# Where q and k of one chunk are turned: by the DMA crossbar behind their load, or on TensorE

## The chip, the cores and the metric

The kernel runs on one core of a Trainium2 chip. The metric is the time of one execution on the device, in microseconds (us). The kernel before was run 11 times: the median is 215.7 us, the lowest 214.82 and the highest 217.98. A difference is given against that median.

The core has five engines, each with its own queue of instructions, which it runs in order: PE (TensorE: matmuls, and transposes as matmuls against an identity matrix), DVE (VectorE), ACT (ScalarE), POOL (GpSimd) and SP (SyncE, which here only issues DMAs). All DMAs share 16 DMA engines. A DMA transpose is a DMA that writes its source turned (rows to columns)[...].

## The reference

A decayed linear attention feeds a feed-forward layer. B=4 batches, H=8 heads, S=768 positions, D=64; the layer has 512 inputs and 2048 hidden units.

```
gamma = 1 - 2 ** (-5 - arange(H))
for t in range(S):
    state = gamma * state + einsum('bhd,bhe->bhde', k[:, :, t], v[:, :, t])
    y[:, :, t] = einsum('bhd,bhde->bhe', q[:, :, t], state) / sqrt(D)
x = y with the heads side by side, 3072 tokens x 512
h = x @ w_in                      # 512 -> 2048
g = h + sin(alpha * h) ** 2 / (alpha + 1e-9)
out = g @ w_out                   # 2048 -> 512, f32
```

## The kernel before, in words

**Chunks.** Positions are cut in chunks of 128; each batch has 6, so there are 24. The list `P` gives the order of work: first the first chunk of each batch (`e0` to `e3`, which are P[0] to P[3]), then the others, batch by batch. P[4] to P[8] are the rest of batch 0, P[9] begins the rest of batch 1. The change is about P[7], the eighth in this order.

**What a chunk goes through.** Its q, k and v are loaded by POOL, three DMAs that cast f32 to bf16 on the way (`load_chunk`, line 83); v is multiplied by decay factors (`scale_v`, line 137). For the scores, q and k have to lie with the head dimension on partitions, so both are transposed: 128 rows of 2 x 512 values become the tile `qkT`. There are two ways for this in the kernel:

- `stage_T` (lines 246 to 251): eight TensorE transposes of 128x128 into one PSUM bank with the tag "ty", and one copy from PSUM to `qkT` on DVE or ACT.
- `turn` (line 256): one DMA transpose, issued by SP, from the loaded tile `qkr` to `qkT`. SP waits for both loads (q and k) before it issues it.

`qkT` has 6 buffers, taken in turn by either way. Then `stage_A` (line 265) computes the scores in small matmuls and DVE masks them (line 269, tile `aT`); `stage_M` (lines 299 and 303) computes the outputs from the state and the scores, adds the chunk to the state (line 279, kept by ACT at line 286), and DVE writes the result to `xT` (line 310). Chunks of the later batches use another layout ("wide") with functions of their own; all of them are turned by DMA.

**Groups and phases.** The feed-forward layer takes the chunks in groups of 4, 2, 4, 4, 4, 4 and 2. A hidden slot (class `Slot`) is matmuls with `w_in` (line 425, tile `ph`), a sine and a square on ACT (lines 428 and 433), and an addition on DVE (line 440, tile `gT`). Matmuls with `w_out` (line 450, tile `po`) of the group before are laid between. A finished tile of 128 tokens is copied by ACT (line 462) and stored by an SP DMA (line 463, `out_dram`). A group's first `ph` matmul needs `xT` of all its chunks.

**Around the change.** The order on each engine is the order in which the code is written (a manual schedule). While the feed-forward of group 1 runs (`phase(1, ...)`, eight steps n = 0 to 7 of two slots each), the attention of P[6] to P[9], which make group 2, is spread over its steps:

```
    phase(1, outs,
          {0: [X(P[8])], 1: [A(P[6])], 2: [T(P[7]), X(P[9])], 3: [A(P[7]), M(P[6])], 4: [X(P[10])],
           5: [A(P[8]), M(P[7])], 6: [X(P[11]), A(P[9]), M(P[8]), SK(e1)], 7: [M(P[9])]}, 2)
```

X is `turn`, T is `stage_T`, A is `stage_A`, M is `stage_M`. So of these four chunks P[6], P[8] and P[9] are turned by DMA and P[7] on TensorE. P[6]'s `turn` is written before the last `w_out` matmuls of the tiles 0 and 1. SP's queue before is: the turn of P[6], the stores of output tiles 0, 1 and 2, then the turns of P[8], P[9], P[10] and P[11], the store of tile 3, and so on. POOL's queue has the loads of P[7], P[8], P[9] and so on, with scalings of v between them, each of which waits for its v.

Of the kernel before, what the change touches and what calls it, by code (L numbers as in the profile page):

```python
# [15 lines left out]
def kernel(  # L16
# [52 lines left out]
    def chunk_of(t, j):  # L69
        b, c = divmod(j, NCH)  # L70
        return t[b, :, c * C:(c + 1) * C, :].rearrange("h s d -> s h d")

    def load_chunk(j, names="qkv"):
        for name, src in (("q", q), ("k", k), ("v", v)):
            if name not in names:
                continue
            if name == "v":
                t = big.tile([128, H, D], BF16, name="vr", tag="vr", bufs=NJ - 9)
            else:
                if ("qk", j) not in raw:  # L80
                    raw["qk", j] = big.tile([128, 2, H, D], BF16, name="qkr", tag="qkr", bufs=NJ - 10)
                t = raw["qk", j][:, "qk".index(name)]
            nc.gpsimd.dma_start(out=t, in_=chunk_of(src, j))  # L83
            raw[name, j] = t

    def wide(j):
        return j >= 2 * NCH + 2 and j != 3 * NCH
# [45 lines left out]
    def scale_v(j, eng):  # L133
        t, by = raw["v", j], kg
        if wide(j):
            t, by = t.rearrange("i f p d -> i (f p) d"), kgq
        eng.tensor_mul(t, t, by[:, j % NCH, :, None].to_broadcast([128, H, D]))  # L137
# [103 lines left out]
    def stage_T(j, eng=None, tag="ty"):  # L241
        pt = psum.tile([128, 2 * NP, 128], BF16, name="pt", tag=tag, bufs=4 if tag == "mm" else 1)
        st["qkT", j] = work.tile([128, 2 * NP, 128], BF16, name="qkT", tag="qkT", bufs=6)
        for i in range(2):
            for p in range(NP):
                nc.tensor.transpose(pt[:, i * NP + p, :],
                                    raw["qk"[i], j][:, 2 * p:2 * p + 2, :].rearrange("p h d -> p (h d)"), ident)
        if eng is nc.scalar:
            nc.scalar.copy(st["qkT", j], pt)
        else:  # L250
            nc.vector.tensor_copy(st["qkT", j], pt)

    def turn(j):

        st["qkT", j] = work.tile([128, 2 * NP, 128], BF16, name="qkT", tag="qkT", bufs=6)
        nc.sync.dma_start_transpose(out=st["qkT", j], in_=raw["qk", j].rearrange(
            "i a f p d -> i (a f p d)" if wide(j) else "i a h d -> i (a h d)"))

    def stage_A(j):
        qkT = st["qkT", j]  # L260
        pa = psum.tile([128, 2, NP, 128], F32, name="pa", tag="pa")
        for p in range(NP):
            for e in range(2):
                r = slice(64 * e, 64 * e + 64)
                nc.tensor.matmul(pa[:, e, p, :], qkT[r, NP + p, :], qkT[r, p, :],  # L265
                                 start=(p == 0), stop=True, skip_group_check=True)
        aT = work.tile([128, 2, NP, 128], BF16, name="aT", tag="aT", bufs=2)
        m = dec.rearrange("p e n t -> p (e n) t") if j % NCH == 0 else mask_bc
        nc.vector.tensor_mul(aT.rearrange("p e n t -> p (e n) t"), pa.rearrange("p e n t -> p (e n) t"), m)  # L269
        st["aT", j] = aT  # L270
# [17 lines left out]
    def stage_M(j):  # L288
        c = j % NCH
        g, i = place[j]  # L290
        if g not in xT:
            xT[g] = work.tile([128, KS, sizes[g] * C], BF16, name="xT", tag="xT", bufs=3)
        qkT, aT, vs = st["qkT", j], st["aT", j], raw["v", j]
        py = psum.tile([128, NP, 128], F32, name="py", tag="ty")
        if c > 0:
            for p in range(NP):
                for e in range(2):
                    r = slice(64 * e, 64 * e + 64)
                    nc.tensor.matmul(py[r, p, :], s_bd[c % 2][:, p, r], qkT[:, p, :],  # L299
                                     start=(p == 0), stop=True, skip_group_check=True)  # L300
        for p in range(NP):
            for e in range(2):
                nc.tensor.matmul(py[64 * e:64 * e + 64, p, :], vs[:, 2 * p + e, :], aT[:, e, p, :],  # L303
                                 start=(c == 0 and p == 0), stop=True, skip_group_check=True)
        x = xT[g][:, :, i * C:(i + 1) * C]
        if c == 0:
            nc.scalar.copy(x, py)
            return
        ps = stage_S(j) if c < NCH - 1 else None
        nc.vector.tensor_mul(x, py, qg[:, c])  # L310
        if ps is not None:
            keep_S(j, ps)
# [229 lines left out]
    def phase(g, outs, att, nf=1):  # L542


        no, done = len(outs), 0
        for n in range(FF // nf):
            more, fresh = rest[0], {}
            now = Slot(g, n * nf, nf=nf).sq("A")
            run(more, "keep", "exit", "hand")
            for fn in att.get(n, ()):  # L550
                fresh.update(fn() or {})
            run(fresh, "mask")
            if fresh:
                rest[0] = fresh
            now.add()
            while done < no * (n + 1) * nf // FF:
                outs[done]()
                done += 1

    def T(j):  # L560
        return lambda: stage_T(j)

    def X(j):
        return lambda: turn(j)

    def A(j):
        return lambda: stage_A(j)

    def M(j):
        return lambda: stage_M(j)  # L570

    def SK(j):
        return lambda: keep_S(j, stage_S(j))
# [3 lines left out]
    P = order  # L577
# [82 lines left out]


    load_chunk(P[7])
    load_chunk(P[8])
    scale_v(P[6], nc.gpsimd)
    load_chunk(P[9])
# [24 lines left out]
    def fill(n):  # L690
        for _ in range(n):
# [9 lines left out]
    stage_M(P[5])  # L701
    fill(4)
    phase(1, outs,
          {0: [X(P[8])], 1: [A(P[6])], 2: [T(P[7]), X(P[9])], 3: [A(P[7]), M(P[6])], 4: [X(P[10])],
           5: [A(P[8]), M(P[7])], 6: [X(P[11]), A(P[9]), M(P[8]), SK(e1)], 7: [M(P[9])]}, 2)

    where = {10: (2, 1)}
# [69 lines left out]
```

## Time and profile before

| | |
|---|---|
| median of 11 runs | 215.7 us |
| the profiled execution | 215.21 us |
| its span, from the first to the last instruction | 213.4 us |
| what lies around the span | 1.8 us |
| TensorE clock granted | 1.00 |
| PE busy | 201.9 us (95%) |
| ACT busy | 159.8 us (75%) |
| DVE busy | 132.1 us (62%) |
| POOL busy | 103.4 us (48%) |
| DMA queue of POOL (loads) | 13.38 MB, 77360 packets |
| DMA queue of SP (transposes, stores) | 11.28 MB, 23808 packets |
| DMA transposes | 17, of which 8 from `qkr` and 9 from the wide tiles |

The page of a profile has a row of busy tenths for each engine over 40 equal slices of the span (here 5.3 us each), a row for the DMA engines, the chain of work that ended last, and the groups of instructions with their durations. Finer views list instructions in order of time, with the idle time before one and what ended it ("0.29 <-DMA qkT" means 0.29 us idle until a DMA into qkT landed). PEld is the weight load that goes ahead of each matmul; SPq marks an instruction of SP's queue. A DMA's duration in such a list is the issuing engine's time alone; the time to landing is given apart.

### The profile page before, as it was taken

The numbers are of one execution on the slowest core, as the hardware profiler recorded it, in microseconds if no ns is written. First come the engines' busy times: TensorE is split into PE (matmuls) and PEld (weight loads), VectorE is DVE, ScalarE is ACT, GpSimd is POOL, SyncE is SP. The second block draws the span as 40 slices with busy tenths as digits, with TensorE's granted clock in tenths as the row PEclk, the third lists the DMA queues.
The fourth block names the chain that finished last, engine by engine and source line by source line (L and its number), as shares of the span: only waits on it lengthen the run. The fifth ranks groups of instructions, "written<-read, shape, count | busy, mean of one in ns | idle before, by whom it ended". The sixth has DMA issues, their size and how long they took to land.

```text
span 213.4 us, 4667 instructions
## 1 busy us (share of the span) xinstructions
PE 201.9 (95%) x1822; PEld 109.1 (51%) x1849; DVE 132.1 (62%) x250; ACT 159.8 (75%) x302; POOL 103.4 (48%) x136
## 2 busy tenths in 40 slices
PE   7898999899989999999999999999999999999994
PEld 2444554457664555554554554554545444665653
DVE  4787859975896777756655756765744644433311
ACT  7688696758889998897697787677678687766630
POOL 8975434899679969999995103303300100000000
PEclk9999999999999999999999999999999999999999
DMA  9999999999999999999999343141011101111112
GB/s 129 146 183 183 206 207 176 154 144 231 169 140 207 127 148 195 93 185 173 173 146 164 92 98 79 22 101 51 0 51 52 48 1 52 49 49 52 49 49 98
DMA packets 101189, 24.95 MB, mean 117 GB/s; under 512 B 93728, under 2 KB 98224, under 8 KB 101168
## 3 DMA queue, kind: packets, MB, share of 16 engines
q0 software_dynamic: 77360, 13.38, 82.4%
q1 hardware_dynamic: 23808, 11.28, 25.0%
q8 instruction: 14, 0.23, 0.4%
q14 instruction: 7, 0.06, 0.1%
HBM read 27.27 MB, written 6.29 MB: 157 GB/s over the span
## 4 chain that ended last, share of the span: by engine, by line
PE 80%; DVE 8%; ACT 7%; issue 3%; DVEq 0%; ACTq 0%
PE po L450 33%; PE ph L425 33%; ACT s L428 4%; DVE aT L269 3%; PE spare L491 3%; DVE gT L440 2%; ACT s L433 2%; PE pa L265 2%; PE poh L473 2%; PE py L299 1%; PE py L303 1%; PE pa L337 1%; PE py L327 1%; DVE xT L310 1%; PE ps L279 1%
## 5 line engine op out<-in xcount | busy, mean ns | idle before, releaser
L440 DVE SCALAR_TENSOR_TENSOR gT<-s,rec_alpha,ph 128x512 bf16<-128x512 f32 (+3 forms) x120 | 74.3, 638 | 64.6 <-ACT s L433 64.3
L425 PE MATMUL ph<-xT,w_in 128*128 128x512 bf16 (+3 forms) x479 | 97.9, 336 | 0.6 <-DVE gT L440 0.2
L428 ACT ACTIVATE s<-ph,alpha_sb 128x512 f32<-128x512 f32 (+3 forms) x120 | 69.5, 601 | 33.8 <-PE ph L425 33.5
L450 PE MATMUL po<-w_out,gT 128*128 128x512 bf16 x343 | 90.6, 379 | 3.3 <-issue 2.5
L425 PEld LDWEIGHTS <-w_in 128*128 128x128 bf16 x480 | 45.6, 98 | 41.9 <-issue 1.1
L433 ACT ACTIVATE s<-s 128x512 f32<-128x512 f32 (+1 forms) x94 | 58.4, 621 | 2.6
L450 PEld LDWEIGHTS <-gT 128*128 128x128 bf16 x368 | 33.9, 98 | 36.4 <-issue 0.6
L391 POOL CAST s_bd<-s_f 64x256 bf16<-64x256 f32 x10 | 3.9, 394 | 40.3 <-DVE s_f L384 30.1
L462 ACT COPY o_sb<-po 128x512 f32<-128x512 f32 x23 | 13.2, 579 | 4.0 <-PE po L450 3.9
L83 POOL DMA_DIRECT2D vr<-in_v_dram x15 | 13.7, 914 | 3.0 <-DMA w_in<-in_moe_w_in_dram 1.7
L83 POOL DMA_DIRECT2D qkr<-in_q_dram x14 | 12.8, 913 | 3.9 <-DMA w_out<-in_moe_w_out_dram 1.7
L137 POOL TENSOR_TENSOR vr<-vr,kg 128x512 bf16<-128x512 bf16 x12 | 12.7, 1072 | 4.0 <-DMA vr<-in_v_dram 3.5
L83 POOL DMA_DIRECT2D qkr<-in_k_dram x14 | 12.5, 892 | 4.0 <-DMA w_out<-in_moe_w_out_dram 3.3
L269 DVE TENSOR_TENSOR aT<-pa,mask 128x1024 bf16<-128x1024 f32 x11 | 13.4, 1219 | 0.5 <-PE pa L265 0.5
L103 POOL DMA_DIRECT2D qk_seq<-in_q_dram x16 | 11.3, 762 | 1.9 <-DMA vr<-in_v_dram 1.2
L103 POOL DMA_DIRECT2D v_seq<-in_v_dram x16 | 11.3, 796 | 0.0
L137 POOL TENSOR_TENSOR v_seq<-v_seq,kgq 128x512 bf16<-128x512 bf16 x9 | 9.6, 1107 | 3.6 <-DMA v_seq<-in_v_dram 3.3
L103 POOL DMA_DIRECT2D qk_seq<-in_k_dram x16 | 11.3, 775 | 0.0
L491 PE MATMUL spare<-warm 128*128 128x512 bf16 x27 | 9.7, 482 | 1.3 <-DVE warm L156 1.2
L286 ACT CAST s_bd<-ps 64x256 bf16<-64x256 f32 x24 | 8.7, 361 | 2.3 <-PE ps L279 2.1
L346 DVE TENSOR_TENSOR aTw<-pa,maskq 128x768 bf16<-128x768 f32 x9 | 8.6, 954 | 0.7
L310 DVE TENSOR_TENSOR xT<-py,qg 128x512 bf16<-128x512 f32 x11 | 7.5, 684 | 1.2 <-PE py L303 1.2
(92 smaller groups left out, 142.8 us busy)
## 6 DMA issues: line engine op xcount, KB each, us to landing
out_dram<-o_sb SPq DMA_DIRECT2D x23, 256.0 KB, 2.3
w_in<-in_moe_w_in_dram POOLq DMA_DIRECT2D x4, 512.0 KB, 11.2
w_out<-in_moe_w_out_dram POOLq DMA_DIRECT2D x4, 512.0 KB, 14.9
vr<-in_v_dram POOLq DMA_DIRECT2D x15, 128.0 KB, 6.9
qkr<-in_q_dram POOLq DMA_DIRECT2D x14, 128.0 KB, 7.0
qkr<-in_k_dram POOLq DMA_DIRECT2D x14, 128.0 KB, 7.0
qk_seq<-in_q_dram POOLq DMA_DIRECT2D x8, 80.0 KB, 6.3
qk_seq<-in_k_dram POOLq DMA_DIRECT2D x8, 80.0 KB, 4.4
```

The source lines that it names most:

```text
L83: nc.gpsimd.dma_start(out=t, in_=chunk_of(src, j))
L103: nc.gpsimd.dma_start(out=o, in_=src[bt, h, cs[0] * C:, :].rearrange("(f i) d -> i f d", i=64))
L137: eng.tensor_mul(t, t, by[:, j % NCH, :, None].to_broadcast([128, H, D]))
L269: nc.vector.tensor_mul(aT.rearrange("p e n t -> p (e n) t"), pa.rearrange("p e n t -> p (e n) t"), m)
L310: nc.vector.tensor_mul(x, py, qg[:, c])
L425: nc.tensor.matmul(self.ph[:, m, :], w_in[:, i, f * 128:(f + 1) * 128], xT[g][:, i, self.lo:self.hi], start=(m == 0 and i == 0), stop=(i = ...
L428: nc.scalar.activation(out=self.s[:, m, :], in_=self.ph[:, m, :], func=ACTF.Sin, scale=alpha_sb[:, f:f + 1])
L433: nc.scalar.activation(out=self.s, in_=self.s, func=ACTF.Square)
L440: nc.vector.scalar_tensor_tensor(gT[self.g][:, f, self.lo:self.hi], self.s[:, m, :], rec_alpha[:, f:f + 1], self.ph[:, m, :], op0=ALU.mult ...
L450: nc.tensor.matmul(po[g, ts], gT[g][:, f, ts * C:(ts + 1) * C], w_out[:, f, :], start=(f == 0), stop=(f == FF - 1))
L462: nc.scalar.copy(o_sb, po[g, ts])
L491: nc.tensor.matmul(spare["ps"], warm[:, :128], warm, start=True, stop=True)
```

## The change

P[7] is turned by a DMA transpose that SP issues, written right behind the chunk's loads. The TensorE transposes and the DVE copy of step n = 2 are left out. The order of the others stays as it was.

```diff
     load_chunk(P[7])
+    turn(P[7])
     load_chunk(P[8])
     scale_v(P[6], nc.gpsimd)
...
     phase(1, outs,
-          {0: [X(P[8])], 1: [A(P[6])], 2: [T(P[7]), X(P[9])], 3: [A(P[7]), M(P[6])], 4: [X(P[10])],
+          {0: [X(P[8])], 1: [A(P[6])], 2: [X(P[9])], 3: [A(P[7]), M(P[6])], 4: [X(P[10])],
            5: [A(P[8]), M(P[7])], 6: [X(P[11]), A(P[9]), M(P[8]), SK(e1)], 7: [M(P[9])]}, 2)
```

On PE this takes out eight transposes with their weight loads, on DVE one copy of 128x1024. On SP one DMA transpose comes in, after the stores of tiles 0 and 1 and before the store of tile 2, which is followed by the turn of P[8]. POOL's and ACT's queues are the same as before. P[7] takes the second buffer of `qkT` and P[8] the third; before, it was the other way round.

## The prediction

> **What bounds the kernel now.** I read the page first, then the chain of work that ended last, then what stands in front of the instructions around the change, last the DMA engines. The page:
>
> ```profile
> PE 201.9 (95%) x1822; PEld 109.1 (51%) x1849; DVE 132.1 (62%) x250; ACT 159.8 (75%) x302; POOL 103.4 (48%) x136
> ...
> DMA  9999999999999999999999343141011101111112
> ```
>
> PE is the bound of the whole, at 95%. The DMA engines are busy in every slice of the first 22, until 117 us. The change sits at 46 to 65 us, in that part: there a transfer takes its time from another.
>
> The chain, in order of time, from P[7]'s present transpose to the start of group 2 (start, duration, what):
>
> ```profile
> 52.55 0.78 DVE gT L440 x2
> 53.33 0.61 DVE qkT L251
> 53.94 0.05 issue
> 53.99 0.40 PE pa L265 x8
> ...
> 63.96 0.65 DVE xT L310
> 64.61 0.04 issue
> 64.65 1.02 PE ph L425 x4
> ```
>
> Phase 1 is a chain through DVE, PE and ACT and not PE work end to end; it ends with P[9]'s `xT`, behind which PE begins group 2 at 64.65. From there PE fills the time (4.00 of 4.00 us in the stretch from 66 to 70), so what phase 1 ends later, the kernel ends later. What PE's queues wait for in it, from the timeline:
>
> ```profile
> 53.99 0.40 PE L265 MATMUL pa<-qkT 64*128 64x128 bf16 x8 [0.22 <-DVE qkT L251]
> 57.80 0.23 PEld L265 LDWEIGHTS <-qkT 64*128 64x128 bf16 x8 [0.29 <-DMA qkT<-qkr]
> 60.61 0.23 PEld L265 LDWEIGHTS <-qkT 64*128 64x128 bf16 x8 [0.59 <-DMA qkT<-qkr]
> ```
>
> These are the scores of P[7], P[8] and P[9]. The last two wait for their DMA transposes: these land at the last moment. SP's own timeline has the issues, to which I add the time to landing that each has when it is asked for alone:
>
> ```profile
> 49.24 1.28 SPq L256 DMA_TRANSPOSE qkT<-qkr  x1
> ...
> 54.01 1.23 SPq L256 DMA_TRANSPOSE qkT<-qkr  x1
> ```
>
> P[8]: 49.24 + 8.5 = 57.75, used at 57.80. P[9]: 54.01 + 6.56 = 60.57, used at 60.61. Slack 0.05 and 0.04 us. P[6] (43.15 + 6.7 = 49.85) is used at 50.20. Later ones have more: P[10] 1.7 us, P[13] 1.6, P[15] 0.9, from P[16] on over 6.
>
> **What goes away.** Eight PE transposes: 0.61 us as modelled, 0.45 from the first to the next matmul (51.85 to 52.30). The DVE copy: 0.69 us, of which 0.61 on the chain. Without both, PE could start P[7]'s scores behind the `ph` matmuls before them, 0.45 earlier than these end now (53.77), at about 53.3 and not 53.99: 0.7 us at most. [...] The row shows them pipelined at 0.45, and the row decides. Whichever it is, this time can't reach the end: the scores of P[8] wait for a DMA at 57.75 that nothing here brings forward. So the saving counts as 0; were P[8] and P[9] not held by DMA, it would be worth up to 0.7.
>
> **What comes in: SP's part.** P[7]'s k is issued at 38.83 and lands 6.9 us later, at 45.8; SP has issued the store of tile 1 by 45.9. The turn starts there and holds SP for 1.24 us, to 47.1. Behind it stands the store of tile 2, which is ready only at 48.74, and then P[8]'s turn. So SP's queue is covered by 1.6 us; a k landing later than that would push the store and P[8]'s turn by the excess. POOL's queue is not changed. The `qkT` buffers that P[7] and P[8] now take belonged to e1 and e2, read long before.
>
> **What comes in: the DMA engines' part.** On SP's DMA queue the new transpose lies behind P[6]'s (landing 49.85) and the stores of tiles 0 and 1 (landing 51.2) and ahead of the store of tile 2 and of P[8]'s transpose. These engines have no room:
>
> ```profile
> 50.00:54.00 4.00, 3.62 (x40) 2.57 (x39) 3.46 (x7) 3.53 (x8) 3.55 (x4) 1.00 2.01 220
> 54.00:58.00 4.00, 3.83 (x59) 2.94 (x60) 3.22 (x6) 3.34 (x9) 2.65 (x3) 1.00 1.97 156
> ```
>
> Behind the stretch stand its length, the busy time of PE, PEld, DVE, ACT and POOL with instructions in brackets, and the granted clock; the last two columns are the busy share of the DMA engines (over 1, since packets overlap on an engine) and GB/s. From 54 to 58 us only loads and a transpose ran, 156 GB/s. A transpose writes 128 x 1024 x 2 bytes = 0.262 MB: 0.262 / 156 GB/s = 1.7 us of all engines. One q load (0.131 MB) is 0.8 us by the same rate.
>
> Ends for its cost. Upper: P[8]'s and P[9]'s transposes, both queued, land 2.8 us apart (57.75, 60.57), which is a transpose and about one load between. [...] even alone, at 131 us, a transpose takes 3.1 us from issue to landing with 1.3 of it on SP. I take 2.1 us: the 1.7 of the transpose and half of a load that gets its turn in between. It is nearer to the 1.7 row, which is the same kind of DMA in the same stage.
>
> **Where the delay goes.** P[7]: its transpose follows the stores at 51.2, so it lands at about 53 to 54.5 (its fellows take 6.4 to 8.5 us from issue, which from 45.9 is 52.3 to 54.4). Its scores start between 53.3 and 54.5: at best 0.7 gained, at worst 0.5 lost, both hidden by the next wait. P[8]: lands at 57.75 + 2.1 = 59.85, the scores start 2.05 later than now. PE stands there, and in its queue behind it stand `M` of P[7], `po` matmuls and the `ph` of step 6; ACT and DVE run dry with it. P[9]: its transpose lies behind P[8]'s, so 60.57 + 2.1 = 62.7. From its scores to the start of group 2, PE's order (scores, `M` of P[8], two `po`, eight `ph`, `M` of P[9], `xT`) takes 64.65 - 60.61 = 4.04 us as now. Group 2 starts at 66.7, 2.0 later. The loads behind are late by about as much as PE is, so P[10] and later keep their slack.
>
> **Sum.** Saving 0, delay +2.0: 215.2 + 2.0 = 217.2 for the profiled execution. This stands 0.5 under the median of the runs, so 215.7 + 2.0 = 217.7 us.
>
> **The rivals.** *Absorbed, no change (the other side).* On the 16 engines the new transpose may take its turn from loads rather than from P[8]'s transpose, for example in the dip at 47.4 to 48 us, where the engines moved half as much. It decides at P[9]'s landing: under 1.1 us later, no difference can be told; unmoved, the 0.7 us saved at P[7] still end at the wait for P[8], and the time is 215.0 to 216.5. For it: P[9]'s loads have slack of their own, and the dip. Against it: one queue in order, P[8] behind P[7], and slack of 0.05.
>
> *Faster.* Only if P[8] and P[9] landed earlier too, with the saving of 0.7 passed on, and a later PE gap closed: 214.5. Nothing in the order of SP or POOL does that.
>
> *More than the transpose.* A load more gets ahead at each turn (the 2.8 us row), POOL, which waits for v before it loads on, falls behind PE, and the chunks with little slack (P[13], P[15] with 0.9) wait a second time: 2.8 + 0.5 to 1, so 219.0 to 219.5.
>
> *Late at P[7] itself.* P[8] needs 3.8 us behind P[7]'s scores (53.99 to 57.80). P[7] would have to land after 56.1 to be what holds P[8] at 59.85. It ends at the same time, 217.7 to 218.5, by another wait.
>
> **How the numbers follow.** P[8] and P[9] pushed by 1.1 to 2.8 us: 0.58. More than that: 0.10. Late at P[7]: 0.07. Absorbed: 0.18. Faster: 0.07. A measurement of this kernel tells 0.5%, 1.1 us, from no change. Slower by over that: 0.58 + 0.10 + 0.07 = 0.75; within it 0.18; faster 0.07. The range goes from 215.5, an absorbed case, to 219.3; the likeliest case's own is 216.8 to 218.6.
>
> **What would show it.** Right: no L246 on PE and no L251 on DVE at 52 to 54; a ninth DMA transpose from `qkr`, issued at about 45.9; P[8]'s scores at about 59.9 and P[9]'s at 62.7, both with an idle wait for the DMA into `qkT`, in sum some 2 us more of it; `ph` of group 2 at 66.7; the same spans behind it. Wrong: P[9]'s scores at 60.6 or earlier, or a start of group 2 at 64.65 or earlier (absorbed), new DMA waits of PE after 70 us (more than the transpose), or P[8]'s scores late without a wait of their own for a DMA (late at P[7]).

## The result and the profile after

The changed kernel takes 218.44 us in the median of 12 runs, against 215.53 us for the kernel before beside it (47 runs). The ratio is 1.0119, with a 95% interval of 1.0096 to 1.0143, and leaves out three of the 12 runs, of 220.6 to 221.1 us, as slow. By this ratio the change costs 2.6 us (2.1 to 3.1). The profiled execution took 218.54 us, its span is 216.8 us (213.4 before).

The page of the changed kernel, first its engines, then the DMA engines over the 40 slices, then the chain that ended last, by engine and by line:

```profile
PE 200.8 (93%) x1814; PEld 107.9 (50%) x1841; DVE 131.2 (61%) x249; ACT 160.1 (74%) x302; POOL 103.4 (48%) x136
...
DMA  9999999999999999999999940331011011111112
...
PE 72%; DMA 14%; POOL 4%; ACT 4%; issue 2%; DVE 2%; POOLq 0%; DVEq 0%; ACTq 0%
PE po L450 32%; PE ph L425 31%; DMA qkT<-qkr 7%; DMA qkr<-in_k_dram 5%; DMA qkT<-qk_seq 2%; POOL qkr L83 2%; ACT s L428 2%; PE poh L473 2%; PE pa L265 2%; PE py L299 1%; POOL vr L83 1%; PE pa L337 1%; PE py L303 1%; PE py L327 1%; ACT s L433 1%
```

PE has eight matmuls fewer and DVE one instruction fewer: the transposes and the copy are gone. The time is longer all the same. The chain now runs through DMAs for 14%, which had no share that the page listed before. Of these, 5% are a load at 10 to 21 us, ahead of anything that differs; the other 9% are transposes into `qkT`. The timeline of PE in the changed kernel has the scores of P[6], P[7], P[8] and P[9], each with its wait:

```profile
52.09 0.40 PE L265 MATMUL pa<-qkT 64*128 64x128 bf16 x8 [0.96 <-DMA qkT<-qkr]
...
56.74 0.40 PE L265 MATMUL pa<-qkT 64*128 64x128 bf16 x8 [1.54 <-DMA qkT<-qkr]
...
60.75 0.40 PE L265 MATMUL pa<-qkT 64*128 64x128 bf16 x8 [0.20 <-DMA qkT<-qkr]
...
63.81 0.40 PE L265 MATMUL pa<-qkT 64*128 64x128 bf16 x8 [0.56 <-DMA qkT<-qkr]
```

All four wait for a DMA transpose. The chain in order of time, from the issue of P[7]'s transpose to the start of group 2:

```profile
47.02 9.68 DMA qkT<-qkr
56.70 0.04 issue
56.74 0.40 PE pa L265 x8
...
58.35 5.42 DMA qkT<-qkr
63.77 0.05 issue
63.81 0.40 PE pa L265 x8
...
66.92 0.70 DVE xT L310
67.62 0.04 issue
67.67 1.02 PE ph L425 x4
```

Two transposes, P[7]'s with 9.68 us and P[9]'s with 5.42, take the place of DVE and ACT work on the chain. P[9]'s is issued at 58.35 and not at 54.01: SP waits for P[9]'s k, which lands 11.5 us behind its own issue (7.8 before). Group 2 starts at 67.67 and not at 64.65. Not all of these 3.0 us belong to the change: this execution was 0.9 us late by the scores of P[4] at 41.16 (40.30 before), ahead of anything that differs. P[6]'s transpose was issued 0.69 us late (43.84, before 43.15). I therefore count from this issue to the start of group 2: 21.50 us before, 23.83 after, 2.3 us more.

The last 0.4 us comes later. Behind 68 us two weight loads of PE wait for a DMA into `qkT`, those of P[13] and P[15]. First the kernel before, then the changed one:

```profile
82.54 0.23 PEld L265 LDWEIGHTS <-qkT 64*128 64x128 bf16 x8 [0.42 <-issue]
94.72 0.11 PEld L337 LDWEIGHTS <-qkT 64*64 64x64 bf16 x4 [0.42 <-issue]
...
85.55 0.23 PEld L265 LDWEIGHTS <-qkT 64*128 64x128 bf16 x8 [0.42 <-DMA qkT<-qkr]
98.15 0.11 PEld L337 LDWEIGHTS <-qkT 64*64 64x64 bf16 x4 [0.84 <-DMA qkT<-qk_seq]
```

PEld stands idle for 0.42 us at both places in the kernel before too, without a DMA. So P[13] loses nothing here (its matmuls have no wait), and P[15] loses 0.4 us. From the start of group 2 to the end of the span it is 149.1 us, before 148.75.

### The profile page after: what moved, and what is told of

It reads as the page before. It is cut to its first block, busy times and chain, and to the rows that moved or that the text cites. A ratio compares the mean times of both kernels' runs of the same rounds, so it can differ in the third digit from the quotient of the medians.

```text
span 216.8 us, 4652 instructions
## 1 busy us (share of the span) xinstructions
PE 200.8 (93%) x1814; PEld 107.9 (50%) x1841; DVE 131.2 (61%) x249; ACT 160.1 (74%) x302; POOL 103.4 (48%) x136
## 4 chain that ended last, share of the span: by engine, by line
PE 72%; DMA 14%; POOL 4%; ACT 4%; issue 2%; DVE 2%; POOLq 0%; DVEq 0%; ACTq 0%
PE po L450 32%; PE ph L425 31%; DMA qkT<-qkr 7%; DMA qkr<-in_k_dram 5%; DMA qkT<-qk_seq 2%; POOL qkr L83 2%; ACT s L428 2%; PE poh L473 2%; PE pa L265 2%; PE py L299 1%; POOL vr L83 1%; PE pa L337 1%; PE py L303 1%; PE py L327 1%; ACT s L433 1%
## 5 line engine op out<-in xcount | busy, mean ns | idle before, releaser
L462 ACT COPY o_sb<-po 128x512 f32<-128x512 f32 x23 | 13.2, 578 | 4.0 <-PE po L450 3.9
L491 PE MATMUL spare<-warm 128*128 128x512 bf16 x27 | 8.8, 447 | 1.4 <-DVE warm L156 1.2
L265 PE MATMUL pa<-qkT 64*128 64x128 bf16 x120 | 6.0, 219 | 4.3 <-DMA qkT<-qkr 3.3
```

The costliest lines, as they stand in the source:

```text
L462: nc.scalar.copy(o_sb, po[g, ts])
L491: nc.tensor.matmul(spare["ps"], warm[:, :128], warm, start=True, stop=True)
```

## The experiments

Each ratio is to the kernel before, run on the same chip in the same session; "us" behind it is the ratio times 215.5.

**The saving alone.** The transpose of P[7] is left out of the computation, and its scores use P[6]'s tile.

```diff
-          {0: [X(P[8])], 1: [A(P[6])], 2: [T(P[7]), X(P[9])], 3: [A(P[7]), M(P[6])], 4: [X(P[10])],
+          {0: [X(P[8])], 1: [A(P[6])], 2: [lambda: st.update({("qkT", P[7]): st["qkT", P[6]]}), X(P[9])], 3: [A(P[7]), M(P[6])], 4: [X(P[10])],
```

> P[7] is transposed nowhere: its scores use the transposed tile of P[6], so P[7]'s transpose is left out of the computation. It shows the saving alone. Engine-time theory: 0 to 0.3 us faster, since P[8] still waits for its DMA. If the saving is on the path: 0.7 us faster.

Measured: 0.9997 (0.9977 to 1.0017), nothing. PE in this kernel reaches P[7]'s scores earlier and then stands before P[8]'s:

```profile
53.59 0.40 PE L265 MATMUL pa<-qkT 64*128 64x128 bf16 x8
...
58.20 0.40 PE L265 MATMUL pa<-qkT 64*128 64x128 bf16 x8 [0.81 <-DMA qkT<-qkr]
```

The wait grew to 0.81 us: the saving is passed to it and ends there, as predicted.

**The DMA transpose alone.** P[7] stays on TensorE, and a DMA transpose of its tile goes to a spare tile in the place of the change. It was run twice, the second time beside the changed kernel.

```diff
     load_chunk(P[7])
+    spare_T = big.tile([128, 2 * NP, 128], BF16, name="spare_T")
+    nc.sync.dma_start_transpose(out=spare_T, in_=raw["qk", P[7]].rearrange("i a h d -> i (a h d)"))
     load_chunk(P[8])
```

> P[7] stays on TensorE as before, and a DMA transpose of the same tile goes to a spare tile that nobody reads, at the place where the change has it. Engine-time theory (the transpose's time on the DMA engines holds up the transposes and loads behind it; the saving on PE and DVE is worth nothing): slower by 2.0 to 2.9 us, as much as the change; the scores of P[8] and P[9] late by 2 us with waits for the DMA into qkT, none at P[7]. Own-landing theory (only the late landing of P[7]'s own transpose, 56.7 us in the changed kernel, costs the time): 0 to 0.5 us, since P[7]'s scores do not wait for the spare.

> The extra transpose that nobody reads, again, P[7] on TensorE: slower by 1.3 to 2.4 us as before. If it equals the changed kernel, the whole of the loss is the engines' time; if it is 0.4 us or more under it, the rest is P[7]'s scores waiting for their own transpose.

Measured: 1.0085 (1.0054 to 1.0116) and 1.0076 (1.0055 to 1.0097), 1.8 and 1.6 us. Nobody reads the result, so this is the price of its place on SP's queue and on the DMA engines. SP's queue has little part in it: P[8]'s turn is issued at 49.27 and 49.33 us, as before (49.24), but lands after 9.9 and 10.4 us (8.5 before), and P[9]'s is issued at 58.18 and 57.06 (54.01 before). The second run's PE:

```profile
53.82 0.40 PE L265 MATMUL pa<-qkT 64*128 64x128 bf16 x8 [0.22 <-DVE qkT L251]
59.77 0.40 PE L265 MATMUL pa<-qkT 64*128 64x128 bf16 x8 [2.15 <-DMA qkT<-qkr]
62.36 0.40 PE L265 MATMUL pa<-qkT 64*128 64x128 bf16 x8
```

P[7] goes its old way, and P[8] waits 2.15 us. From P[6]'s issue to group 2 it is 23.6 and 23.2 us in the two runs: as much later as in the changed kernel.

**The changed kernel again**, once beside the experiments that follow below and once beside the extra transpose.

> The changed kernel once more, beside the others on one chip, and with a second profile. In the first profile P[6]'s transpose took 8.2 us to land and the start was 0.9 us late; with the extra transpose that nobody reads it took 6.7. If the change itself slows P[6]'s, it takes about 8 us again; if that was this one execution, 6.7. Engine-time theory with the own landing as a small addition: slower by 2.2 to 2.9 us, 0.3 to 1.1 more than with the extra transpose.

> The changed kernel beside the extra transpose on one chip, to tell what P[7]'s own landing adds to the engines' time. Both: slower by 2.2 to 3.2 us. If the own landing adds nothing: within 0.4 us of the extra transpose. P[6]'s transpose takes 6.7 us to land if the 8.2 of the first profile was that execution alone.

Measured: 1.0150 (1.0101 to 1.0198) and 1.0125 (1.0092 to 1.0158). The profiled execution of the first took 418.71 us and is not read. In the trace of the second P[6]'s transpose takes 6.8 us to land and is not waited for by PE's matmuls, so the 8.2 us and the 0.96 us wait of the first profile don't belong to the change. P[7] waits 2.26 us there, and from P[6]'s issue to group 2 it is 23.35 us. On one chip the changed kernel is 1.0 us slower than the extra transpose in the median (218.08 and 217.12; the intervals of the ratios just touch). In the traces this is not in phase 1, where the two are equal within 0.2 us (means 23.6 and 23.4), but behind it: from group 2 to the end 150.0 us, against 148.7 and 148.8 with the extra transpose. The waits of P[13] and P[15] in this trace:

```profile
86.11 0.23 PEld L265 LDWEIGHTS <-qkT 64*128 64x128 bf16 x8 [1.49 <-DMA qkT<-qkr]
98.55 0.11 PEld L337 LDWEIGHTS <-qkT 64*64 64x64 bf16 x4 [0.68 <-DMA qkT<-qk_seq]
```

Less the usual 0.42, P[13] loses 1.07 us here and P[15] 0.26; together they are the 1.3 us by which this stretch is longer. In all four traces, two of the changed kernel and two with the extra transpose, P[13]'s transpose is issued at 77.1 to 78.1 us and not at 72.8. POOL shows where that begins. It scales P[9]'s v before it issues P[11]'s loads, and this v lands 13.2 us behind its issue in the first trace of the changed kernel (8.4 before). First the kernel before, then the changed one:

```profile
55.35 1.04 POOL L137 TENSOR_TENSOR vr<-vr,kg 128x512 bf16<-128x512 bf16 x1 [1.80 <-DMA vr<-in_v_dram]
...
60.83 1.04 POOL L137 TENSOR_TENSOR vr<-vr,kg 128x512 bf16<-128x512 bf16 x1 [6.60 <-DMA vr<-in_v_dram]
```

The other three traces have 5.8 to 6.1 us there. P[11]'s loads are issued 5.5 us later than before in the first trace, and those behind them wait their turn. P[13]'s transpose has 1.6 us of slack before, and PE itself is 2 to 3 us later. With the extra transpose it still landed in time, by 0.1 and 1.4 us; in the changed kernel it landed in time once (7.1 us behind its issue) and late the other time (8.2 us). Why it took longer in that one trace, with as many DMAs in the queues, stays open.

**The own landing alone.** P[7] by DMA as in the change, and P[8] on TensorE in exchange, so that as many transposes as before go by DMA.

```diff
     load_chunk(P[7])
+    turn(P[7])
...
-          {0: [X(P[8])], 1: [A(P[6])], 2: [T(P[7]), X(P[9])], 3: [A(P[7]), M(P[6])], 4: [X(P[10])],
+          {1: [A(P[6])], 2: [X(P[9])], 3: [A(P[7]), M(P[6])], 4: [T(P[8]), X(P[10])],
```

> P[7] by DMA at the place of the change and P[8] on TensorE in step 4, so three of P[6] to P[9] go by DMA as before, only which ones changes. Engine-time theory: P[9]'s transpose has as many ahead of it as before, so within 0.7 us of before. Own-landing theory: P[7] still lands late, so slower by 1 to 2.5 us.

Measured: 1.0077 (1.0049 to 1.0104), 1.7 us, on the side of the rival. Its PE:

```profile
55.73 0.40 PE L265 MATMUL pa<-qkT 64*128 64x128 bf16 x8 [2.06 <-DMA qkT<-qkr]
58.07 0.61 PE L246 MATMUL pt<-ident,qkr 128*128 128x128 bf16 x8
59.91 0.40 PE L265 MATMUL pa<-qkT 64*128 64x128 bf16 x8
```

P[7] alone, waiting 2.06 us for its own transpose, moves group 2 by 1.9 us (23.4 from P[6]'s issue). P[8] on TensorE by itself costs nothing (0.9998, below). So there are two causes, each enough by itself: P[7]'s late landing, and the delay of P[8] and P[9]. They lie one behind the other in the same stretch of PE's queue, and so they don't add up.

**A later place.** P[7]'s turn behind the store of tile 2, right ahead of P[8]'s.

```diff
-          {0: [X(P[8])], 1: [A(P[6])], 2: [T(P[7]), X(P[9])], 3: [A(P[7]), M(P[6])], 4: [X(P[10])],
+          {0: [X(P[7]), X(P[8])], 1: [A(P[6])], 2: [X(P[9])], 3: [A(P[7]), M(P[6])], 4: [X(P[10])],
```

> P[7] by DMA, but issued behind the store of tile 2 and right ahead of P[8]'s transpose, some 2 us later than in the change. Engine-time theory: slower by 2 to 2.9 us as with the change, whatever the place; P[6]'s transpose, which landed 2.2 us later in the changed kernel, back to a landing within 7 us of its issue. Own-landing theory: P[7] lands 2 us later still, so slower by 3.5 to 4.5 us.

Measured: 1.0241 (1.0207 to 1.0275), 5.2 us. The own landing decides here:

```profile
57.50 0.61 PE L265 MATMUL pa<-qkT 64*128 64x128 bf16 x8 [3.80 <-DMA qkT<-qkr]
62.75 0.40 PE L265 MATMUL pa<-qkT 64*128 64x128 bf16 x8
65.18 0.40 PE L265 MATMUL pa<-qkT 64*128 64x128 bf16 x8
```

P[8] and P[9] no longer wait for a DMA; PE, held 3.80 us at P[7], comes to them late. The 5.2 us are more than the 3.5 to 4.5 expected. The landing is not the whole of it: from the end of this wait on, the granted clock of TensorE is 0.50 for about 3 us (the rows are in the last section). From P[7]'s scores to group 2 it takes 12.2 us, where the swap takes 10.7.

**Without P[6]'s transpose ahead.** P[7] by DMA as in the change, P[6] and P[8] on TensorE.

```diff
-    turn(P[6])
...
     load_chunk(P[7])
+    turn(P[7])
...
-          {0: [X(P[8])], 1: [A(P[6])], 2: [T(P[7]), X(P[9])], 3: [A(P[7]), M(P[6])], 4: [X(P[10])],
+          {0: [T(P[6])], 1: [A(P[6])], 2: [X(P[9])], 3: [A(P[7]), M(P[6])], 4: [T(P[8]), X(P[10])],
```

> P[7] by DMA as in the change, but P[6] (step 0, where DVE stands idle) and P[8] (step 4) on TensorE, so no transpose lies ahead of P[7]'s in SP's queue. Engine-time theory: P[7] lands by 53.5 and is not waited for, one DVE copy fewer in the tight part than with P[7] and P[8] on TensorE; within 0.5 us of before, at best 0.5 faster. If P[7]'s landing is late even with a free queue (54.5 or later), slower by 1 to 2 us like the kernel with P[7] and P[8] swapped.

Measured: 1.0029 (1.0014 to 1.0044), 0.6 us. P[7]'s transpose, issued at 45.83 us with only two stores ahead of it on SP's queue, asked for alone:

```profile
L256 SPq DMA_TRANSPOSE qkT<-qkr x1: 1351/1351/1351, 45.8 to 45.8; - x1
...
DMA to landing us min/median/max: 9.2/9.2/9.2
```

It still lands after 9.2 us, at 55.06, and PE waits 1.36 us. P[6]'s transpose is thus not what makes it late. The cost is less than the 1 to 2 us that were expected for so late a landing.

**The same bytes, not turned.** A plain copy to a spare tile in the same place.

```diff
     load_chunk(P[7])
+    spare_C = big.tile([128, 2, H, D], BF16, name="spare_C")
+    nc.sync.dma_start(out=spare_C, in_=raw["qk", P[7]])
     load_chunk(P[8])
```

> Before, with a plain DMA copy of P[7]'s q and k to a spare tile in the place of the new transpose: the same 0.262 MB, not turned. If bytes or a place in the queue cost the time: slower by 1.2 to 1.9 us, like the extra transpose (1.8). If it is the turning: within 0.7 us of before[...].

Measured: 1.0035 (1.0010 to 1.0060), 0.75 us, under half of the transpose's 1.6 to 1.8, though the intervals touch. So the turning seems to cost about as much again as the bytes and the place in the queue do. It is not what makes the landing late: the copy, issued at 47.0 us, takes 8.3 us to land. The profiled execution took 217.06 us, over the median of 216.06; in it P[8]'s transpose takes 9.7 us, nearly as long as beside the extra transpose.

**Two of them.** A second spare transpose behind the first.

```diff
     load_chunk(P[7])
+    spare_T = big.tile([128, 2 * NP, 128], BF16, name="spare_T")
+    nc.sync.dma_start_transpose(out=spare_T, in_=raw["qk", P[7]].rearrange("i a h d -> i (a h d)"))
+    spare_T2 = big.tile([128, 2 * NP, 128], BF16, name="spare_T2")
+    nc.sync.dma_start_transpose(out=spare_T2, in_=raw["qk", P[7]].rearrange("i a h d -> i (a h d)"))
     load_chunk(P[8])
```

> Two extra transposes to two spare tiles in the same place, P[7] on TensorE. Engine-time theory: the second costs at least as much as the first, as it falls on engines that have no room left: slower by 4 to 6 us. If the first one's cost is a disturbance that comes once (a wait that the queue has anyway): 1.8 to 2.5 us, about as with one.

Measured: 1.0265 (1.0224 to 1.0306), 5.7 us. The second costs 4.0 us, more than twice the first. P[8]'s scores wait twice as long as with one:

```profile
61.94 0.40 PE L265 MATMUL pa<-qkT 64*128 64x128 bf16 x8 [4.40 <-DMA qkT<-qkr]
```

Counted from P[6]'s issue, they start 2.3 to 2.5 us later than with one, about what the first cost there (1.9 to 2.1). The rest lies behind this wait, where the granted clock is 0.50 from 62.8 to 66.1 us: from these scores to group 2 it takes 7.8 us, and 6.5 in the trace with one extra transpose that is shown above. So the experiment does not show that a second transpose costs the DMA engines twice the first.

**Fewer by DMA than before.** P[8], or else P[9], on TensorE beside P[7].

```diff
-          {0: [X(P[8])], 1: [A(P[6])], 2: [T(P[7]), X(P[9])], 3: [A(P[7]), M(P[6])], 4: [X(P[10])],
+          {1: [A(P[6])], 2: [T(P[7]), X(P[9])], 3: [A(P[7]), M(P[6])], 4: [T(P[8]), X(P[10])],
```

```diff
-          {0: [X(P[8])], 1: [A(P[6])], 2: [T(P[7]), X(P[9])], 3: [A(P[7]), M(P[6])], 4: [X(P[10])],
+          {0: [X(P[8])], 1: [A(P[6])], 2: [T(P[7])], 3: [A(P[7]), M(P[6])], 4: [T(P[9]), X(P[10])],
```

> The other direction: P[8] goes to TensorE as well as P[7] (step 4), one DMA transpose fewer than before. Engine-time theory: P[9]'s transpose has one fewer ahead of it and lands 2 to 3 us earlier, no score waits for a DMA in phase 1; faster by 0.3 to 1.0 us, as far as the chain through DVE allows. If phase 1 is bound by DVE and PE alone: slower by 0.5 to 1.3 us, the price of the transposes and the copy.

> P[9] to TensorE in step 4, P[7] too as before, P[8] by DMA. Engine-time theory: P[8] still waits to 57.75, the scores of P[9] no longer wait; group 2 starts up to 0.3 us earlier, so faster by 0 to 0.5 us. If PE and DVE bound phase 1 alone: slower by 0.5 to 1.3 us.

Measured: 0.9998 (0.9980 to 1.0017) and 1.0013 (0.9991 to 1.0036): no gain, and no loss of the price of the transposes either. With P[8] on TensorE the chain ends phase 1 like this:

```profile
61.77 1.13 DVE aT L269
62.90 0.60 DVE xT L310
63.50 0.78 DVE gT L440 x2
64.28 0.65 DVE xT L310
64.93 0.04 issue
64.97 1.02 PE ph L425 x4
```

No wait for `qkT` by DMA is left in phase 1, and yet group 2 starts at 64.97, 21.85 us behind PE's scores of P[5]; before it is 21.86. In phase 1 of the kernel before, the transfers and the chain through DVE end at nearly the same time: moving one more transpose to TensorE gains nothing (0.9998 and 1.0013), adding one to the DMA engines costs at once (1.8 and 1.6 us).

No kernel here beats the one before.

## Why the prediction was right, point by point

The forecast was 217.7 us, 2.0 slower; it is 2.6 slower (2.1 to 3.1).

*What goes away counts 0.* Right, and shown: the saving alone is 0.9997, and its interval leaves out more than 0.5 us.

*P[8] and P[9] are pushed by 2.1 us.* Right in size, and for P[8] mostly by the way that was given: its transpose is 1.4 to 1.5 us longer on the way, and it is issued 0.3 to 0.8 later. From P[6]'s issue, P[8] landed at 14.6 us before and at 16.9 and 16.3 in the two traces of the changed kernel, 2.3 and 1.7 later; P[9] at 17.4, then 19.9 and 19.5, 2.5 and 2.0 later. Group 2 was to start 2.0 later and started 2.3 and 1.9 later by the same count. The price taken from the row of 156 GB/s, 1.7 us, came out for a transpose (1.8 and 1.6 us for the one that nobody reads), but not for the same bytes unturned (0.75 us for the plain copy). P[9] got there by another way. I had its transpose land late because it lies behind P[8]'s. In the trace it is issued 3.7 and 3.2 us later by the same count, since its k lands late, and it then lands faster than before (5.4 us, before 6.6). So the two transfers that I took for an upper end, P[8]'s and P[9]'s landings 2.8 us apart, did not show what a transpose costs: there too SP had waited for P[9]'s k. That P[9]'s delay came out near 2.1 is partly luck.

*P[7] lands at 53 to 54.5.* Wrong. Its transpose takes 9.1 to 9.7 us and not 6.4 to 8.5, and so PE waits at P[7] first, 1.5 to 2.3 us. I had taken its fellows' times. The number of transposes in the queue is not the reason, since with P[6]'s and P[8]'s gone it still took 9.2. This made no difference to the sum of phase 1, because P[8]'s delay would have held PE as long. The swap shows that it would have cost the time alone: the rival "late at P[7]", to which I gave little, is as much of a cause as the step that I chose.

*SP is held for 1.24 us.* Too short: 2.3 and 2.5 us in the changed kernel, and P[8]'s turn behind it 3.9 and 3.5 (1.28 before). In the first trace P[7]'s turn ended on SP at 49.33 and the store of tile 2 was issued at 49.60, so the cover was just enough.

*The loads behind are late by about as much as PE is, so later chunks keep their slack.* Wrong, and it is where the forecast is short. P[15] in one trace, P[13] and P[15] in the other wait a second time, 0.4 us of the span in the first and 1.3 in the second. I had this as a part of the rival "more than the transpose", with the same two chunks and the same way, POOL's wait for v. P[11]'s loads and P[13]'s transpose are issued 5 us later than before, while PE is only 2 to 3 us late.

*A lower clock* stood in no part of the forecast. Of the nine executions in the ratio, five have a mean granted clock of 0.998 or more and a mean time of 217.9 us; four have 0.991 or 0.992 and 218.6. In the experiments' executions of the kernel before, 103 in all, it is never under 0.998. So part of the 2.6 us is likely the clock. No trace of the changed kernel with the lower clock was kept, so where it falls is not shown.

*Absorbed.* Fell by its own sign: P[9] landed 2.5 and 2.0 us later, and not under 1.1.

## What to carry to other kernels

Here, with the DMA engines busy at 90% or more in every slice of the page until 117 us, a DMA transpose cost in two places: with its time on the engines, at the readers of the transfers queued behind it (1.8 and 1.6 us with the extra transpose), and with its own way to landing, 9.1 to 9.7 us, at its own reader (1.7 us with the swap). Either was enough to cost the time, so look at the slack of both before work is moved off the matmul engine; here the slack of P[8]'s and P[9]'s transposes was 0.05 and 0.04 us. And the saving on PE and DVE was worth nothing here (0.9997), since the next scores in PE's queue waited for a DMA.

## What the runs showed of the hardware that was not expected

*The clock behind a long wait.* The granted clock is the share of TensorE's full speed that the profile shows. The pages of the kernels with two extra transposes and with the later place have, in this order, these rows of the granted clock over the 40 slices (5.5 us each):

```profile
PEclk9999999999979999999999999999999999999999
...
PEclk9999999999799999999999999999999999999999
```

Read more finely, the clock is 0.50 from about 62.8 to 66.1 us in the first, where PE's wait of 4.40 us ends at 61.94, and from about 57.3 to 60.5 in the second, where one of 3.80 ends at 57.50. In these stretches eight `ph` matmuls take 1.91 us in the first (1.04 before it) and two `po` matmuls 1.03 in the second (0.59 before it). No other trace read here has such a stretch; the longest wait for `qkT` in them is 2.36 us. All nine executions of these two kernels have a mean clock of 0.984 to 0.992. So each time a long wait of PE was followed by some 3 us at half clock, which cost about 1.4 and 1.5 us by the counts given with these experiments. Which length of wait brings it was not measured.

*The DMA engines moved less, not more.* From 44 to 68 us of the kernel before and of the changed kernel (length; busy time of PE, PEld, DVE, ACT and POOL; granted clock; DMA share; GB/s):

```profile
44.00:68.00 24.00, 22.43 (x293) 15.16 (x297) 17.89 (x31) 19.09 (x43) 20.39 (x22) 1.00 1.95 175
```

```profile
44.00:68.00 24.00, 19.74 (x276) 13.81 (x280) 16.73 (x27) 16.94 (x40) 17.34 (x19) 1.00 1.76 158
```

175 GB/s before, 158 after, 160 in its second trace. Part of it is that fewer loads were there: POOL issued P[11]'s 5.5 us later, at 61.81 us, and at the end of the row below the engines stand almost idle. Another part are stretches in which the engines stand although loads are queued, as in the changed kernel from 44 to 64 us, in slices of 0.5 us:

```profile
DMA  9999999519999999999999999999999999999901
GB/s 120 132 112 129 153 155 96 41 10 100 121 134 144 194 284 274 271 262 179 144 155 160 157 206 302 220 159 158 159 160 150 153 155 146 157 174 158 288 7 13
```

At 47.5 to 48.5 us they moved 41 and 10 GB/s, and P[8]'s k, issued at 42.96, had not landed then (it took 7.6 us). The kernel before has a dip in the same place, a smaller one (71 GB/s at 47.5 to 48 us). What holds the engines there is not shown. It may be why a transpose issued at 46 us takes over 9 us, and a plain copy issued at 47 us 8.3, but that was not tried.
